# Packed attention and two dense layers: the second stage in blocks of 496, 496, 496, 320 and 496

## The chip, the cores and the metric

The kernel runs on one core of a Trainium2 chip. The metric is the device time of the program in microseconds. Before the change it is 1392.48 us, the median of three runs (1389.37 to 1394.6).

## What is computed

An attention over 32 packed positions, and behind it two feed-forward layers one after the other, all in float32 accuracy:

```python
p_packed = sm_attn(p, k, v)              # 8 batches, 8 heads, 32 packed rows, 576 tokens, 64 wide
out = sm_attn(q, p_packed, p_packed)     # 576 tokens against the 32 packed rows
x = out -> (4608 tokens, 512)
h = x @ w_in;  x = max(0.01*h, h) @ w_out              # first layer, 512 -> 2048 -> 512
h = x @ w_in2; x = h*sigmoid(1.702*h) @ w_out2         # second layer
```

The weights arrive as float64 and are turned into float32 on the chip.

## The kernel before, in words

Four stages follow one another, and in each TensorE has a long stream of matmuls.

- **First stage** (L563 to L600): attention, and the first activations g1 = leaky relu of x times w_in1. Per batch of 576 tokens there are 16 row groups of 128 features in two halves of 288 tokens; each is six matmuls (L369), then one activation on ScalarE (L378) into a ring of tiles g (L377), four activations to a tile, and one store of the tile to memory (L382). The ring has four buffers. In the last batch no attention work is left.
- **Second stage** (L603 to L698): y = g1 times w_out1. It is done as a Strassen product: seven products instead of eight, over token halves i and feature halves h. The tokens go in five blocks; a block (t0, n) covers 2n tokens, its halves n each. Per block the seven products run in the order of PRODUCTS (L42), each over eight row groups f; a step is one (block, product, f) and issues six matmuls of n columns (L693): two output columns times three terms, since each operand is split into a rounded high part and a low rest (high x high, high x low, low x high).
- **Third stage**: the second layer's activations, in the same manner with six blocks of 768 tokens (L727).
- **Fourth stage**: the second layer's output, again in five blocks (L840), in the order 480, 480, 480, 480, 384.

What sets the order around the change is an agenda (L122 to L145): `at(step, ...)` puts work on a step, `side(step)` issues it there, ahead of the step's matmuls. Each engine works through its own instructions in that order. In the second stage the agenda holds:

- the raw tiles of g1, loaded through SP's queue (L454 to L463), one buffer for each of their names, those of the first block in the last batch of the first stage (L591 to L593);
- the split of every second row group pair: a cast on ScalarE (L499) four steps ahead, the subtraction on VectorE (L140) three steps ahead, into three rotating slots (ROLL, L468); in a slot the high and low parts lie at offsets that depend on n (L496);
- the Strassen combinations of raw tiles on VectorE (L475 to L483), 16 a block, and the evacuation of the products (L516 to L547), copies on ScalarE and five additions on VectorE a block, with four stores of y a block (L611);
- the splits of w_out1's weights, 18 halves in the first block (L442 to L452, L557);
- sixteen conversions of w_in2 to float32 with its combinations (L166 to L196, called at L675): each loads three pieces, works on ScalarE, VectorE (L159, L162, L178 to L182) and POOL (L163), and stores one (L184). A conversion with start s loads in step s and does the rest in steps s + 6 to s + 15, the addition on POOL in s + 8;
- at the end, the first loads and splits for the third stage (y_block, L677), which take over the conversions' buffers: loads in step 240, first use in step 249.

Blocks of the second stage take 56 steps each: the fourth has steps 168 to 223, the fifth 224 to 279.

The parts that the diff touches:

Of the kernel before, what the change touches and what calls it, by code (L numbers as in the profile page):

```python
# [9 lines left out]
F32 = mybir.dt.float32  # L10
# [8 lines left out]
B, H, S, D, J = 8, 8, 576, 64, 32  # L19
# [8 lines left out]

WIDE = 480
ROW = 512  # L30
SLOT = 4 * ROW + 128
BLOCKS = {"b": [(0, 384), (768, 480), (1728, 480), (2688, 480), (3648, 480)],
          "d": [(0, 480), (960, 480), (1920, 480), (2880, 480), (3840, 384)]}
# [45 lines left out]
def packed_attention_moe_moe_kernel(tc, qT, kT, vm, vt, pT, w_in1, w_out1, w_in2, w_out2, out):  # L79
# [31 lines left out]
    with ExitStack() as ctx:  # L111
# [262 lines left out]
        def relu(b, f, hf, t):  # L374
            g = b, f // 2
            if g not in g1t:
                g1t[g], made[g] = pa.tile([P, 2, S], F32, tag="g", name=f"g1_{b}_{f}", bufs=4), 0  # L377
            nc.scalar.activation(g1t[g][:, f % 2, hf * TH:hf * TH + TH], t[:, :TH], AF.Prelu, alpha=0.01)  # L378
            made[g] += 1
            if made[g] == 4:  # L380
                f -= f % 2
                nc.sync.dma_start(g1[f:f + 2, :, b * S:b * S + S].rearrange("f p t -> p f t"), g1t.pop(g))  # L382
# [71 lines left out]
        def load_raw(blk, i, h, fp, nm, g):  # L454
            if blk < NBK:
                home, tag = "dr", f"r{i}{h}{fp}" if i == h else f"r10{fp}"
                if nm == "d":
                    home, tag = ("cy", f"y{fp}") if i != h else ("d" if h else "d0", f"r{i}{h}{fp}")
                t0, n = BLOCKS[nm][blk]
                t = pools[home].tile([P, 2, WIDE], F32, tag=tag, name=f"{nm}r_{blk}_{i}{h}{fp}")[:, :, :n]  # L460
                f0, t0 = NJ * h + 2 * fp, t0 + n * i
                nc.sync.dma_start(t, g[f0:f0 + 2, :, t0:t0 + n].rearrange("f p t -> p f t"))
                raws[blk, i, h, fp] = t  # L463
# [7 lines left out]
        def prepare(nm, g, steps=steps, home_of=split_home):  # L471
# [14 lines left out]
            def high(k, blk, p, f):  # L486
# [7 lines left out]
                else:  # L494
                    t = pools[home].tile([P, SLOT], F32R, tag=tag, name=f"{nm}a_{blk}_{p}_{f}")
                    hi, lo = (bass_rows(t[:, o:], n) for o in ((32, 2 * ROW + 96) if n == WIDE else (0, 2 * ROW)))  # L496
                for c in range(2):
# [18 lines left out]
        def evacuate(k, blk, p, bank, shape, store, home=None):  # L516
            def tile_(what):
                if home:
                    outs[what] = home[:, "uv".index(what), :, :shape[1]]
                else:  # L520
                    outs[what] = pools["d"].tile([P, 2, WIDE], F32, tag=what[0], name=f"{what}_{blk}")[:, :, :shape[1]]
                return outs[what]
# [92 lines left out]
        def y_block(early, steps, blk):  # L615
# [4 lines left out]
            def load():  # L620
                for i, j in ((0, 0), (1, 0), (1, 1), (0, 1)):
# [7 lines left out]
                    else:  # L629
                        home, tag = ("d", "yq") if blk == 0 else ("cy", f"y{2 * i + j}")  # L630
                        q[i, j] = pools[home].tile([P, 2, HB if blk == 0 else WIDE], F32, tag=tag, name=f"yq_{blk}_{i}{j}")[:, :, :HB]
                    nc.sync.dma_start(q[i, j], yT[2 * j:2 * j + 2, :, t0 + HB * i:t0 + HB * i + HB].rearrange("d p t -> p d t"))
# [41 lines left out]
        later_weights(lambda n: "w5" if n < 8 else "d", wo1c, "wo1", 0)  # L674
        combined("wi2", [42 + 23 * i // 2 for i in range(16)], 6)  # L675
        last = 7 * NJ * (NBK - 1)
# [135 lines left out]
        def store_out(blk, i, h, t, columns=(0, 1)):  # L812
            n = BLOCKS["d"][blk][1]
            if 0 in columns:
# [3 lines left out]
                else:  # L818
                    outs["rows"] = pools["d"].tile([P, 2, WIDE], F32, tag="rows", name=f"rows_{blk}_{i}{h}")[:, :, :n]
            for c in columns:  # L820
# [9 lines left out]
        for k, (blk, p, f) in enumerate(last_steps, LATER):  # L830
            if k == LATER + 4:
                uv = pools["cs"].tile([P, SLOT], F32, tag="wj", name="uv")
                uv = uv[:, :4 * WIDE].rearrange("p (i c w) -> p i c w", i=2, c=2)
            side(k)
# [65 lines left out]
```

## Time and profile before

| | before |
|---|---|
| median of three runs | 1392.48 us |
| profiled execution, span | 3422.4 us |
| TensorE busy in it | 3415.1 us |
| VectorE busy | 1064.6 us |
| ScalarE busy | 786.4 us |
| POOL busy | 89.7 us |
| DMA | 302.48 MB, 88 GB/s over the span |

The profile is one execution, taken by the hardware profiler; the page gives its span and no further time for it. Its span is 2.46 times the median of the runs, and readers should keep the two apart: a duration of the profile isn't at once a duration of the timed run. Rows name a line of the kernel, an engine, the operation and its tiles, out <- in; "128x960" is partitions by elements. Busy time is the time in which an engine had an instruction in work. SPq is SP's queue of DMA issues; "to landing" is the time from an issue until its data have arrived. The mean of one matmul in a group covers its overlap with the next, so busy time over count is what one costs in a stream. A window's row gives, for a stretch in us from the span's start, the busy time of each engine with its instructions in brackets, then the granted TensorE clock (PEclk, 1.00 is the 2.4 GHz level), the mean share of the 16 DMA engines that was busy and the GB/s; PEld is TensorE's weight load.

### The profile page before, as it was taken

How to read it: one execution, taken by the hardware profiler on the slowest of the kernel's cores; microseconds unless marked ns; L12 is line 12 of the kernel's file. 1: busy time of each engine (PE TensorE's matmuls, PEld its weight loads, DVE VectorE, ACT ScalarE, POOL GpSimd, SP SyncE). 2: the span in 40 equal slices, each digit the busy share in tenths (PEclk: the TensorE clock that was granted, in tenths of full speed). 3: DMA queues.
4: the chain of work that ended last, by engine and by line, in shares of the span. 5: the costliest groups of instructions: out<-in, count | busy, mean ns of one | idle time of the engine just before them, and what ended most of it. 6: DMA issues, size and time to landing. Idle time of an engine off the chain costs nothing.

```text
span 3422.4 us, 23306 instructions
## 1 busy us (share of the span) xinstructions
PE 3415.1 (100%) x8746; PEld 2461.0 (72%) x8746; DVE 1064.6 (31%) x1548; ACT 786.4 (23%) x1363; POOL 89.7 (3%) x71
## 2 busy tenths in 40 slices
PE   9999999999999999999999999999999999999999
PEld 7788888887666666666777777777766666666677
DVE  5233333233333333332322222321123333233332
ACT  4222222222112111111322222222222111111111
POOL 2000000000000000000000000000000000000000
DMA  6233333433222222211223332322231213031211
GB/s 247 92 133 131 132 131 104 138 111 100 64 86 64 83 78 62 93 45 58 97 87 110 104 106 94 106 96 74 94 122 54 69 29 86 23 86 29 66 32 19
DMA packets 283249, 302.48 MB, mean 88 GB/s; under 512 B 88576, under 2 KB 246272, under 8 KB 283136
## 3 DMA queue, kind: packets, MB, share of 16 engines
q1 hardware_dynamic: 280736, 300.71, 27.4%
q8 instruction: 68, 1.11, 0.1%
q10 hardware_dynamic: 2400, 0.30, 0.1%
q14 instruction: 45, 0.37, 0.0%
HBM read 184.55 MB, written 116.39 MB: 88 GB/s over the span
## 4 chain that ended last, share of the span: by engine, by line
PE 100%; issue 0%; POOL 0%; DVE 0%; ACT 0%; POOLq 0%
PE y L693 26%; PE h L727 26%; PE sum L840 19%; PE h L369 15%; PE first L840 8%; PE m L243 2%; PE s L243 1%; PE keep L389 1%; PE pp L301 1%; PE t L284 1%; PE tr L286 0%; PE t L310 0%; DVE rows L822 0%; POOL ident masks.py:199 0%; ACT ppk L313 0%
## 5 line engine op out<-in xcount | busy, mean ns | idle before, releaser
L727 PE MATMUL h<-ya,wj 128*128 128x384 f32 x2016 | 900.6, 679 | 0.0
L727 PEld LDWEIGHTS h<-ya,wj 128*128 128x128 f32 x2016 | 704.8, 352 | 195.7 <-issue 173.7
L693 PE MATMUL y<-ba,wo 128*128 128x480 f32 (+1 forms) x1080 | 579.9, 769 | 0.0
L369 PEld LDWEIGHTS h<-a,m 128*128 128x128 f32 x1536 | 493.5, 363 | 64.2 <-issue 51.0
L369 PE MATMUL h<-a,m 128*128 128x288 f32 x1536 | 523.3, 565 | 0.0
L693 PEld LDWEIGHTS y<-ba,wo 128*128 128x128 f32 x1080 | 379.6, 352 | 199.1 <-issue 197.2
L840 PE MATMUL sum<-da,wo 128*128 128x480 f32 (+1 forms) x840 | 452.3, 769 | 0.0
L840 PEld LDWEIGHTS sum<-da,wo 128*128 128x128 f32 x840 | 295.1, 352 | 155.5 <-issue 154.0
L693 PE MATMUL y<-ba,wo_early 128*128 128x480 f32 (+1 forms) x600 | 322.7, 768 | 0.0
L140 DVE TENSOR_TENSOR ba<-br,ba 128x960 fp32r<-128x960 f32 (+1 forms) x140 | 156.5, 1118 | 491.3 <-ACT ba L499 491.2
L140 DVE TENSOR_TENSOR da<-dr,da 128x960 fp32r<-128x960 f32 (+1 forms) x139 | 155.0, 1115 | 489.2 <-ACT da L499 489.2
L693 PEld LDWEIGHTS y<-ba,wo_early 128*128 128x128 f32 x600 | 211.0, 352 | 110.3 <-issue 108.9
L499 ACT CAST da<-dr 128x960 fp32r<-128x960 f32 (+1 forms) x139 | 133.3, 961 | 681.9 <-PE sum L840 432.3
L499 ACT CAST ba<-br 128x960 fp32r<-128x960 f32 (+1 forms) x140 | 134.5, 961 | 649.8 <-PE y L693 569.9
L378 ACT ACTIVATE g<-h 128x288 f32<-128x288 f32 x256 | 105.1, 411 | 455.9 <-PE h L369 427.5
L840 PE MATMUL sum<-da,wo_early 128*128 128x480 f32 (+1 forms) x360 | 193.8, 769 | 0.0
L840 PEld LDWEIGHTS sum<-da,wo_early 128*128 128x128 f32 x360 | 126.7, 352 | 66.4 <-issue 65.4
L840 PE MATMUL first<-da,wo 128*128 128x480 f32 (+1 forms) x240 | 129.9, 769 | 0.0
L749 DVE TENSOR_TENSOR g<-v,h 128x384 f32<-128x384 f32 x48 | 26.6, 554 | 331.4 <-PE h L727 331.4
L840 PE MATMUL first<-da,wo_early 128*128 128x480 f32 (+1 forms) x228 | 123.0, 766 | 0.0
L840 PEld LDWEIGHTS first<-da,wo 128*128 128x128 f32 x240 | 84.5, 353 | 43.8 <-issue 43.1
L840 PEld LDWEIGHTS first<-da,wo_early 128*128 128x128 f32 x228 | 79.9, 351 | 42.0 <-issue 41.0
(129 smaller groups left out, 1633.4 us busy)
## 6 DMA issues: line engine op xcount, KB each, us to landing
g_scratch<-g SPq DMA_DIRECT2D x64, 576.0 KB, 3.0
g_scratch<-g SPq DMA_DIRECT2D x96, 384.0 KB, 2.8
br<-g_scratch SPq DMA_DIRECT2D x64, 480.0 KB, 3.9
dr<-g_scratch SPq DMA_DIRECT2D x64, 480.0 KB, 3.7
stage<-wi_scratch SPq DMA_DIRECT2D x72, 256.0 KB, 2.8
wo_scratch<-b_wo SPq DMA_DIRECT2D x32, 448.0 KB, 4.1
k<-in_kT_dram SPq DMA_DIRECT2D x16, 576.0 KB, 4.9
q<-in_qT_dram SPq DMA_DIRECT2D x16, 576.0 KB, 4.8
```

Source lines behind the costliest of these rows:

```text
L140: at(step + 1, lambda: nc.vector.tensor_sub(*rest))
L243: nc.tensor.matmul(tiles[par][32 * i:32 * i + 32, :n], lhsT=lhsT(r, i, par), rhs=rhs(r, i), start=True, stop=True)
L284: nc.tensor.transpose(t[par][:, P * k:P * k + P], e[:, par, P * k:P * k + P], ident)
L301: nc.tensor.matmul(t[32 * i:32 * i + 32, D * par:D * par + D], lhsT=et[:n, par, k, 32 * i:32 * i + 32], rhs=v[:n, i // 2, k, c0:c0 + D], s ...
L369: nc.tensor.matmul(t[:, :TH], lhsT=m[:, ws, par, o:o + P], rhs=a[:, xs, par, :], start=(k == 0), stop=(k == 5))
L378: nc.scalar.activation(g1t[g][:, f % 2, hf * TH:hf * TH + TH], t[:, :TH], AF.Prelu, alpha=0.01)
L389: nc.tensor.matmul(keep[:, :P], lhsT=ident, rhs=ident, start=True, stop=True)
L499: nc.scalar.copy(hi, src)
L693: nc.tensor.matmul(acc[BANK[p]][:, c, :n], lhsT=w[:, ws, P * c:P * c + P], rhs=x[xs], start=(p in OPENS and f + m == 0), stop=(f == NJ - 1 ...
L727: nc.tensor.matmul(to, lhsT=w[:, ws, COMBO[p], P * kk:P * kk + P], rhs=x[:, xs, kk, :], start=(p in UNIT_OPENS and kk + s == 0), stop=(kk ...
L749: nc.vector.tensor_add(g[1][:, HB:], v, d)
L840: nc.tensor.matmul(column_of(acc4[BANK[p]], c)[:, :n], lhsT=w[:, ws, c], rhs=x[xs], start=(p in OPENS and f + m == 0), stop=(f == NJ - 1 a ...
```

## The change

The second stage's blocks become 496, 496, 496, 320, 496 instead of 384, 480, 480, 480, 480 tokens per half, with tiles of 496 where they are the second stage's and 480 where they are the fourth's. The offsets of the parts in a slot go by n > 384 instead of n = 480. The last four conversions start in steps 181, 194, 207 and 220 instead of 180, 191, 203 and 214. The ring of tiles for the first activations has three buffers instead of four.

```diff
--- before.py
+++ after.py
@@ -26,10 +26,10 @@
 TB = 768
 HB = TB // 2
 
-WIDE = 480
+WIDE = {"b": 496, "d": 480}
 ROW = 512
 SLOT = 4 * ROW + 128
-BLOCKS = {"b": [(0, 384), (768, 480), (1728, 480), (2688, 480), (3648, 480)],
+BLOCKS = {"b": [(0, 496), (992, 496), (1984, 496), (2976, 320), (3616, 496)],
           "d": [(0, 480), (960, 480), (1920, 480), (2880, 480), (3840, 384)]}
 NBK = 5
 SCALE = 1.0 / 8.0
@@ -374,7 +374,7 @@
         def relu(b, f, hf, t):
             g = b, f // 2
             if g not in g1t:
-                g1t[g], made[g] = pa.tile([P, 2, S], F32, tag="g", name=f"g1_{b}_{f}", bufs=4), 0
+                g1t[g], made[g] = pa.tile([P, 2, S], F32, tag="g", name=f"g1_{b}_{f}", bufs=3), 0
             nc.scalar.activation(g1t[g][:, f % 2, hf * TH:hf * TH + TH], t[:, :TH], AF.Prelu, alpha=0.01)
             made[g] += 1
             if made[g] == 4:
@@ -457,7 +457,7 @@
                 if nm == "d":
                     home, tag = ("cy", f"y{fp}") if i != h else ("d" if h else "d0", f"r{i}{h}{fp}")
                 t0, n = BLOCKS[nm][blk]
-                t = pools[home].tile([P, 2, WIDE], F32, tag=tag, name=f"{nm}r_{blk}_{i}{h}{fp}")[:, :, :n]
+                t = pools[home].tile([P, 2, WIDE[nm]], F32, tag=tag, name=f"{nm}r_{blk}_{i}{h}{fp}")[:, :, :n]
                 f0, t0 = NJ * h + 2 * fp, t0 + n * i
                 nc.sync.dma_start(t, g[f0:f0 + 2, :, t0:t0 + n].rearrange("f p t -> p f t"))
                 raws[blk, i, h, fp] = t
@@ -493,7 +493,7 @@
                     hi, lo = (bass_rows(x, n) for x in (hi, lo))
                 else:
                     t = pools[home].tile([P, SLOT], F32R, tag=tag, name=f"{nm}a_{blk}_{p}_{f}")
-                    hi, lo = (bass_rows(t[:, o:], n) for o in ((32, 2 * ROW + 96) if n == WIDE else (0, 2 * ROW)))
+                    hi, lo = (bass_rows(t[:, o:], n) for o in ((32, 2 * ROW + 96) if n > HB else (0, 2 * ROW)))
                 for c in range(2):
                     ga[blk, p, f + c] = hi[:, c], lo[:, c]
                 nc.scalar.copy(hi, src)
@@ -518,7 +518,7 @@
                 if home:
                     outs[what] = home[:, "uv".index(what), :, :shape[1]]
                 else:
-                    outs[what] = pools["d"].tile([P, 2, WIDE], F32, tag=what[0], name=f"{what}_{blk}")[:, :, :shape[1]]
+                    outs[what] = pools["d"].tile([P, 2, WIDE["b"]], F32, tag=what[0], name=f"{what}_{blk}")[:, :, :shape[1]]
                 return outs[what]
             if p == 1 and home:
                 u = tile_("u")
@@ -628,7 +628,7 @@
                         q[i, j] = q[home, tag][:, o:o + 2 * HB].rearrange("p (a b) -> p a b", a=2)
                     else:
                         home, tag = ("d", "yq") if blk == 0 else ("cy", f"y{2 * i + j}")
-                        q[i, j] = pools[home].tile([P, 2, HB if blk == 0 else WIDE], F32, tag=tag, name=f"yq_{blk}_{i}{j}")[:, :, :HB]
+                        q[i, j] = pools[home].tile([P, 2, HB if blk == 0 else WIDE["d"]], F32, tag=tag, name=f"yq_{blk}_{i}{j}")[:, :, :HB]
                     nc.sync.dma_start(q[i, j], yT[2 * j:2 * j + 2, :, t0 + HB * i:t0 + HB * i + HB].rearrange("d p t -> p d t"))
 
             def one(i):
@@ -672,7 +672,7 @@
 
         first_raws("b", g1)
         later_weights(lambda n: "w5" if n < 8 else "d", wo1c, "wo1", 0)
-        combined("wi2", [42 + 23 * i // 2 for i in range(16)], 6)
+        combined("wi2", [42 + 23 * i // 2 for i in range(12)] + [181, 194, 207, 220], 6)
         last = 7 * NJ * (NBK - 1)
         y_block(last + 16, [last + k for k in (25, 27, 30, 35, 42, 49, 54)], 0)
         side_until(0)
@@ -816,7 +816,7 @@
                     rows = pools["conv"].tile([P, 4 * HB], F32, tag="cx", name=f"rows_{blk}_{i}{h}")
                     outs["rows"] = rows[:, :2 * n].rearrange("p (c w) -> p c w", c=2)
                 else:
-                    outs["rows"] = pools["d"].tile([P, 2, WIDE], F32, tag="rows", name=f"rows_{blk}_{i}{h}")[:, :, :n]
+                    outs["rows"] = pools["d"].tile([P, 2, WIDE["d"]], F32, tag="rows", name=f"rows_{blk}_{i}{h}")[:, :, :n]
             for c in columns:
                 rows = outs["rows"][:, c]
                 nc.vector.transpose(rows, column_of(t, c)[:, :n])
@@ -830,7 +830,7 @@
         for k, (blk, p, f) in enumerate(last_steps, LATER):
             if k == LATER + 4:
                 uv = pools["cs"].tile([P, SLOT], F32, tag="wj", name="uv")
-                uv = uv[:, :4 * WIDE].rearrange("p (i c w) -> p i c w", i=2, c=2)
+                uv = uv[:, :4 * WIDE["d"]].rearrange("p (i c w) -> p i c w", i=2, c=2)
             side(k)
             x, w = ga.pop((blk, p, f)), wt[p, f // 4][:, :, f % 4].rearrange("p s (c w) -> p s c w", c=2)
             n = BLOCKS["d"][blk][1]
```

## Rows read from the trace of the kernel before

**Rows 1.** The page: span, busy time of each engine, the chain that ended last.
```profile
span 3422.4 us, 23306 instructions
...
PE 3415.1 (100%) x8746; PEld 2461.0 (72%) x8746; DVE 1064.6 (31%) x1548; ACT 786.4 (23%) x1363; POOL 89.7 (3%) x71
...
PE 100%; issue 0%; POOL 0%; DVE 0%; ACT 0%; POOLq 0%
```

**Rows 2.** Stage two by block: us, PE, PEld, DVE, ACT, POOL, PEclk, DMA, GB/s.
```profile
717.15:867.21 150.06, 150.06 (x337) 117.59 (x337) 57.97 (x73) 36.55 (x52) 1.29 (x1) 1.00 0.32 103
867.21:1054.76 187.55, 187.55 (x337) 118.28 (x336) 64.78 (x79) 36.04 (x41) 8.83 (x5) 1.00 0.23 76
1054.76:1242.31 187.55, 187.55 (x337) 118.19 (x336) 64.05 (x75) 36.06 (x41) 8.83 (x5) 1.00 0.24 76
1242.31:1429.86 187.55, 187.55 (x337) 118.34 (x336) 65.16 (x79) 36.03 (x41) 8.04 (x5) 1.00 0.25 79
1429.86:1617.41 187.55, 187.55 (x337) 118.07 (x336) 65.61 (x66) 35.39 (x40) 0.00 (x0) 1.00 0.13 42
```

**Rows 3.** Groups by shape, PE, L693's two shapes | busy us, mean ns.
```profile
L693 PE MATMUL y<-ba,wo 128*128 128x480 f32 x864 | 483.3, 791 | 0.0
...
L693 PE MATMUL y<-ba,wo 128*128 128x384 f32 x216 | 96.7, 680 | 0.0
```

**Rows 4.** Windows by product of the first block of stage two.
```profile
717.15:738.59 21.44, 21.44 (x50) 16.80 (x50) 8.55 (x10) 3.64 (x5) 0.00 (x0) 1.00 0.47 151
738.59:760.02 21.43, 21.43 (x50) 17.08 (x49) 8.52 (x10) 5.07 (x7) 0.00 (x0) 1.00 0.23 69
760.02:781.46 21.44, 21.44 (x49) 16.66 (x48) 8.85 (x11) 6.11 (x9) 0.00 (x0) 1.00 0.33 103
781.46:802.90 21.44, 21.44 (x50) 16.57 (x49) 7.15 (x9) 5.42 (x8) 0.00 (x0) 1.00 0.00 0
802.90:824.34 21.44, 21.44 (x50) 16.92 (x49) 10.58 (x13) 5.41 (x8) 0.00 (x0) 1.00 0.26 87
824.34:845.78 21.44, 21.44 (x49) 17.02 (x48) 7.11 (x9) 6.11 (x9) 0.00 (x0) 1.00 0.56 181
845.78:867.21 21.43, 21.43 (x49) 16.54 (x48) 7.21 (x11) 4.79 (x6) 1.29 (x1) 1.00 0.42 133
```

**Rows 5.** Groups by shape, VectorE, then ScalarE, stage two | busy us, mean ns.
```profile
L140 DVE TENSOR_TENSOR ba<-br,ba 128x960 fp32r<-128x960 f32 x112 | 129.7, 1158 | 416.1 <-ACT ba L499 416.1
L140 DVE TENSOR_TENSOR ba<-br,ba 128x768 fp32r<-128x768 f32 x27 | 25.9, 958 | 73.6 <-ACT ba L499 73.4
...
L140 DVE TENSOR_TENSOR wo<-wo 128x512 fp32r<-128x512 f32 x18 | 11.7, 685 | 0.0
L162 DVE SCALAR_TENSOR_TENSOR raw_wi<-raw_wi 128x512 uint32<-128x512 uint32 x16 | 11.0, 689 | 0.3
L159 DVE TENSOR_SCALAR raw_wi<-raw_wi 128x512 uint32<-128x512 uint32 x16 | 6.9, 429 | 1.0 <-ACT raw_wi L156 1.0
...
L179 DVE TENSOR_TENSOR b_wi<-b_wi 128x128 f32<-128x128 f32 x16 | 4.7, 292 | 0.6
...
L499 ACT CAST ba<-br 128x960 fp32r<-128x960 f32 x112 | 111.2, 993 | 558.5 <-PE y L693 496.9 <-issue 61.6
```

**Rows 6.** End of stage one: its window; lines L378 and L382; DMA issues there.
```profile
645.70:717.15 71.45, 71.45 (x241) 63.19 (x239) 11.05 (x16) 21.23 (x48) 0.00 (x0) 1.00 0.42 140
...
L378 ACT ACTIVATE g<-h x256: 404/411/418, 48.0 to 717.3; 128x288 f32<-128x288 f32 x128
...
L382 SPq DMA_DIRECT2D g_scratch<-g x64: 359/377/517, 64.0 to 717.8; - x64
...
DMA to landing us min/median/max: 2.9/3.0/6.6
...
g_scratch<-g SPq DMA_DIRECT2D x8, 576.0 KB, 3.3
br<-g_scratch SPq DMA_DIRECT2D x12, 384.0 KB, 4.8
```

## The prediction

> **What bounds the kernel now.** I read the page first. TensorE is busy for 3415.1 of a span of 3422.4 us, and the chain that ended last is 100% PE [rows 1]. In the profiled execution nothing but the matmul stream counts. Its span is 2.46 times the median of the timed runs (3422.4 / 1392.48), and the page gives no other time for it. So the sum is made on that execution and carried over: if every matmul shrinks alike, a profiled microsecond is worth 0.407 us in the timed runs.
>
> Next the windows, one for each block of the second stage [rows 2]. The block of 384 tokens takes 150.06 us, each block of 480 takes 187.55. Divided by the width that is 0.3908 and 0.3907 us per token of width. There is no fixed part: a block costs its width and nothing else. The per-shape groups agree, 483.3 us / 864 = 559 ns for 480 columns and 96.7 / 216 = 448 ns for 384 [rows 3]. Every window shows a granted clock of 1.00, the 2.4 GHz level [rows 2], so no gated stretch explains the slow matmuls.
>
> Then the other engines in the same windows. VectorE is busy 57.97 us in the first block and 64.05 to 65.61 in the others, ScalarE 35 to 37 [rows 2]. Against 150 or 187 us that is far from bounding. But the timed runs went through the same work 2.46 times faster, and VectorE's and ScalarE's instructions don't shrink with TensorE's. Carried over, the first block gives TensorE 150.06 x 0.407 = 61.1 us against VectorE's 57.97, and a block of 480 has 76.3 against 65. So VectorE is close behind TensorE, closest in the first block, and there the change works. The seven products of that block show where VectorE's load gathers: 10.58 us in the fifth, 7.1 to 8.9 in the others [rows 4].
>
> **The change, part by part.**
>
> *Block widths, TensorE.* The widths sum to 384 + 4 x 480 = 2304 before and 4 x 496 + 320 = 2304 after; each block issues 336 matmuls either way. At 0.3907 us per token of width the stage costs 900.2 us in the profiled execution before and after: difference 0. This is the term that sits on the path.
>
> *Block widths, VectorE and ScalarE.* Each block has 28 splits (L140), 16 combinations (L475 to L483) and 5 additions of the evacuation (L532 to L546), 49 instructions over twice the width. L140's takes 1158 ns at 960 elements and 958 at 768 [rows 5], and I take that for all 49, so 1.04 ns per element: 1191 at 992, 825 at 640. The first block therefore gains 49 x 0.233 = 11.4 us, each block going from 480 to 496 gains 1.6, the one that falls to 320 loses 16.3. The instruction count and the elements are the same in sum. The renamed widths and the test n > 384 leave the fourth stage's tiles and every slot's kind of offset as they were: 0. ScalarE's cast goes the same way (993 ns at 960 [rows 5], some 1020 at 992); its 37 us a block stay off the path.
>
> *Conversions.* The last four of the 16 start at steps 181, 194, 207, 220 instead of 180, 191, 203, 214. Counting steps, one whole conversion leaves the fourth block for the fifth. On VectorE it costs 0.429 + 0.689 + 4 x 0.29 = 2.3 us [rows 5]. It also takes its three loads and one store on SP's queue and its addition on POOL with it, later by 1 to 6 steps. Its last store now falls in step 235, and the next user of its buffers, the loading for the third stage, issues in step 240. Should that cover fail, that load waits on SP's queue with the loads behind it, and the first reader comes in step 249. I take 0.
>
> *VectorE per block after* (from [rows 2] and the two terms above): 69.4, 66.4, 65.7, 46.6, 69.5 us, sum 317.6 as before. At the carried-over pace TensorE has 78.9 us for a width of 496 and 50.9 for 320. TensorE stays longer in every block: gain 0.
>
> *What if TensorE is faster in the timed runs than 0.407 of the profile, with waits making up the rest?* No row shows that pace, so I bound it from both sides. Let c be TensorE's time per token of width. A block costs the longer of c x width and VectorE's time. The carried-over c is 0.159; VectorE's time per token of width is 0.151, 0.135, 0.133, 0.136, 0.137 before and 0.140, 0.134, 0.132, 0.146, 0.140 after. Above 0.151 the change gives 0. Between 0.146 and 0.151 only the old first block waits for VectorE, and the gain grows to 2.1 us. From there to 0.140 the new block of 320 waits too, and the gain grows slowly to 11.37 - 64 x 0.140 = 2.4 us. Below that the new first and fifth blocks wait as well: at 0.137 the change loses 5.5 - 6.2 = 0.7 us. With TensorE free of charge both kernels cost VectorE's 317.6: 0 again. So by whole blocks the change is worth between 0.7 us lost and 2.4 us gained, whatever the pace.
>
> The Trainium skill has a pace in "TensorE: Matmul & The Clock Gate", section "Back-to-back issue gap": N/2.4 + 2.5 ns for a warm matmul. The 559 ns of [rows 3] at a granted clock of 1.00 don't agree with its 202.5; no row here shows it for the timed runs. By it the old first block would have 54.6 us of matmuls against 57.97, the new fourth 45.6 against 46.6, and the sum would be a gain of 2.4 us, an estimate of 1390.1.
>
> *Three buffers instead of four (L377).* A buffer is filled by four activations, stored, and free once the store has landed. In the last eighth of the first stage, where nothing else runs, a fill takes 71.45 / 8 = 8.93 us in the profile [rows 6], 3.6 carried over. Fill, activation 0.41, issue 0.38 and landing 3.0 make 7.4 us against 3 x 3.6 = 10.9 until its next use; with the longest landing of the trace, 6.6 us [rows 6], 11.0. I take 0. The cover is the time in which the other two buffers fill; without it the activation waits, then TensorE for its bank. The upper end is a rival below. A gain is excluded: a ring with fewer buffers waits no less.
>
> *Larger first loads.* Twelve raw tiles of the first block are fetched in that same eighth, 384 KB each [rows 6], now 496: 1.3 MB more. There DMA ran at a share of 0.42 and 140 GB/s, so 333 GB/s when full: 4.1 us more transfer, after 0.42 x 71.45 = 30 us. At the timed pace that eighth lasts 29 us. The first block of the second stage absorbs it (48 us of transfer at share 0.32 [rows 2], in 61 before and 79 after), and the last of these tiles are first read in step 9. I take 0, bounds 0 and +4.1; a gain is excluded, since no byte less moves.
>
> *Sum.* 0 at the carried-over pace, up to 2.4 gained; I take 1.5, because the first block is where both bounds meet and some of the timed run must be waiting. 1392.5 - 1.5 = **1391.0 us**, no change. A measurement of this kernel tells about 0.5% (7 us) from nothing.
>
> **Rivals.**
>
> *A: the old first block stalls by product, not by block.* VectorE can work only a few steps ahead, since the split values have three slots. If no lead carries over at all, each product costs the longer of the two. At c = 0.140 a product of 384 has 7.69 us; the excesses of [rows 4] add to 0.86 + 0.83 + 1.16 + 2.89 = 5.7 us, at 0.130 to 8.1. If the wider block hides all that and the block of 320 pays nothing, the time is 1385. For it: the weight splits (18 of 0.69 us) all fall in this block. Against it: products of 7.1 stand on both sides of the 10.58, and the block of 320 has VectorE at 0.146 of its own. Chance 0.2.
>
> *B: the end of the first stage (slower).* With transfers filling that eighth, stores land late, and with three buffers the activation waits for them. The price per tile is a third of what fill + 0.79 + landing exceeds three fills. At a fill of 3.6 us, 7 us over 8 tiles needs landings of 9.1 us; at 2.9 us (c = 0.140), 7.6. With 4.1 us of transfers exposed as well it gives up to +9: 1399 to 1401. For it: DMA demand of 30 us in 29. Against it: a median landing of 3.0, the rest of the stage has slower fills, and loads queued late aren't needed until the second stage. Chance 0.14.
>
> *C: it does only what the widths say.* TensorE bounds every block in the timed runs too; 1392.5. This is the forecast's own lower end, counted with it: 0.66 together.
>
> **How the numbers follow.** Forecast 0.66, 1388 to 1394 by itself. Range: down to 1381 for A beyond its price and the unshown handoffs, up to 1400 for B's middle. Faster by over 0.5% needs 1385.5 or less: A, 0.20. Slower needs 1399.4 or more: B, 0.14. Same: 0.66.
>
> **What would show it.** In a profile of the same kind: windows of about 194 us for the blocks of 496 and 125 for 320; VectorE near 69, 66, 66, 47, 69; four POOL additions of the second stage in the fourth block and one in the fifth; activations of L378 waiting only for TensorE. If TensorE shows idle time before L693 there, or L378 waits for a store, A's or B's mechanism is at work. The prediction is wrong if the time leaves 1385.5 to 1399.4; a profile in which matmuls run at another pace would settle c.

## The result and the profile after

The changed kernel is **slower by 17.8 us**: a median of 1409.83 us (1406.27 to 1411.17, four runs) against 1391.99 (1389.37 to 1394.6, four runs), ratio 1.0122 with a 95% interval of 1.0102 to 1.0142. The prediction said no change, 1391.0, and its range ended at 1400.

The profiled execution after ran at the pace of the timed runs (it is the one of 1406.27 us), and so did a second profiled execution of the kernel before, called *before again* below (experiment 1). They can be compared directly; the first profile of before, with its span of 3422.4 us [rows 1], can't. The two spans differ by 14.9 us and not by 17.8, since the profiled execution after is the fastest of its four runs. The page of after, span and busy time:

```profile
span 1404.5 us, 23312 instructions
...
PE 1369.8 (98%) x8746; PEld 1218.8 (87%) x8746; DVE 1056.2 (75%) x1548; ACT 767.2 (55%) x1363; POOL 94.8 (7%) x71
```

The same lines of before again. VectorE is busy for 76% of the span, not the 31% of [rows 1]:

```profile
span 1389.6 us, 23306 instructions
...
PE 1363.6 (98%) x8746; PEld 1225.7 (88%) x8746; DVE 1052.7 (76%) x1548; ACT 768.4 (55%) x1363; POOL 97.9 (7%) x71
```

The windows of after (columns as in [rows 2]): first the last batch of stage one, then the five blocks of stage two, with widths 496, 496, 496, 320, 496:

```profile
293.00:324.80 31.80, 30.36 (x243) 26.47 (x241) 9.55 (x15) 18.85 (x46) 0.00 (x0) 1.00 1.02 377
...
324.80:401.20 76.40, 75.66 (x337) 63.17 (x337) 70.33 (x74) 43.48 (x55) 1.30 (x1) 1.00 0.66 222
401.20:477.20 76.00, 76.00 (x337) 63.08 (x336) 67.86 (x78) 36.96 (x41) 11.06 (x5) 1.00 0.60 195
477.20:553.20 76.00, 76.00 (x337) 63.08 (x336) 67.14 (x77) 36.31 (x41) 9.03 (x5) 1.00 0.55 170
553.20:614.90 61.70, 54.55 (x337) 52.24 (x336) 50.09 (x77) 26.69 (x39) 6.57 (x4) 0.94 0.59 192
614.90:691.70 76.80, 75.56 (x338) 62.80 (x337) 67.90 (x69) 37.30 (x42) 2.14 (x1) 1.00 0.38 129
```

The same windows of before again, widths 384 and four times 480:

```profile
294.50:323.90 29.40, 29.26 (x242) 26.40 (x241) 10.45 (x15) 19.75 (x48) 0.00 (x0) 1.00 1.04 379
...
323.90:383.70 59.80, 58.87 (x338) 58.29 (x337) 55.26 (x68) 36.87 (x53) 1.81 (x1) 1.00 0.73 240
383.70:458.20 74.50, 74.15 (x339) 62.61 (x338) 65.68 (x84) 36.23 (x41) 12.68 (x5) 1.00 0.64 207
458.20:531.30 73.10, 73.10 (x337) 62.95 (x336) 66.95 (x78) 36.13 (x41) 8.95 (x5) 1.00 0.62 202
531.30:604.90 73.60, 73.60 (x337) 62.82 (x337) 66.15 (x80) 36.11 (x41) 9.19 (x5) 1.00 0.61 201
604.90:678.60 73.70, 73.70 (x336) 62.65 (x335) 64.25 (x66) 35.55 (x40) 0.94 (x1) 1.00 0.32 108
```

TensorE still costs its width and nothing else where it isn't kept waiting: 76.0 / 496 = 0.1532 us per token, 73.6 / 480 = 0.1533. Five blocks without a wait would be 2304 x 0.1533 = 353.2 us. Before again has 354.7, after 366.9. Of the 13.7 us too many, 12.6 lie in one block: a width of 320 is 49.0 us of matmuls and took 61.7. TensorE is idle there for 7.15 us, and its matmuls take 54.55, which is 5.5 us more than 49.0. The last three stretches of that block show where part of those 5.5 us is, in the column before the last two, the granted clock:

```profile
593.00:601.00 8.00, 7.24 (x39) 7.24 (x40) 7.58 (x13) 2.32 (x4) 0.02 (x1) 0.79 0.70 202
601.00:609.00 8.00, 6.24 (x40) 5.75 (x40) 3.00 (x5) 3.54 (x6) 0.18 (x1) 0.99 1.06 377
609.00:614.90 5.90, 5.90 (x32) 5.79 (x31) 5.08 (x9) 2.04 (x2) 1.11 (x1) 0.72 1.05 392
```

After TensorE had stood idle, part of the following stretch was granted at the 1.2 GHz level: means of 0.79 and 0.72, worth some 0.21 x 8.0 + 0.28 x 5.9 = 3.3 us (an estimate from these rows). The wide blocks show 1.00. So a wait can be paid for twice. Not each one is: in the four windows of 8 us before these, from 561 to 593, TensorE was idle for 4.6 us in all, and the clock stayed at 1.00.

What TensorE waited for is in the waits of that block (us in total, times, longest):

```profile
ACT raw_wi L155 <- DMA raw_wi<-in_w_in_dram: 8.5, 4, 3.9
DVE raw_wi L159 <- ACT raw_wi L156: 8.3, 3, 4.3
PEld y L693 <- DVE ba L140: 7.6, 7, 2.6
PE y L693 <- DVE ba L140: 5.8, 6, 2.3
```

Read from the bottom: TensorE waits for split values of VectorE (5.8 us), and, in the top line, ScalarE waits for the loads of a conversion (8.5 us). Before again has, in its second to fourth blocks together, 3.4 us of ScalarE's waits for such loads and 0.3 us of TensorE's for VectorE. The timeline of one conversion in the narrow block, the one that starts in step 181, ties them together (start, duration, engine, instruction; in square brackets the wait before it):

```profile
562.76 1.78 POOL L163 TENSOR_TENSOR b_wi<-raw_wi 128x512 int32<-128x512 int32 x1 [11.15 <-DVE raw_wi L162]
...
567.46 0.29 DVE L182 TENSOR_TENSOR b_wi<-b_wi 128x128 f32<-128x128 f32 x1
...
567.82 0.56 SPq L184 DMA_DIRECT2D wi_scratch<-b_wi  x1
...
568.55 1.53 SPq L173 DMA_DIRECT2D raw_wi<-in_w_in_dram  x2
570.13 0.60 SPq L174 DMA_DIRECT2D raw_wi<-in_w_in_dram  x1
...
574.00 0.67 ACT L155 ACTIVATE raw_wi<-raw_wi 128x512 int32<-128x512 uint32 x1 [2.03 <-DMA raw_wi<-in_w_in_dram]
...
575.12 2.12 ACT L499 CAST ba<-br 128x640 fp32r<-128x640 f32 x3
...
576.33 0.82 DVE L140 TENSOR_TENSOR ba<-br,ba 128x640 fp32r<-128x640 f32 x1
...
577.20 2.02 PE L693 MATMUL y<-ba,wo 128*128 128x320 f32 x12 [0.62 <-DVE ba L140]
...
577.88 1.75 POOL L163 TENSOR_TENSOR b_wi<-raw_wi 128x512 int32<-128x512 int32 x1 [13.35 <-DVE raw_wi L162]
...
578.40 1.93 DVE L140 TENSOR_TENSOR ba<-br,ba 128x640 fp32r<-128x640 f32 x1
...
580.38 0.85 PE L693 MATMUL y<-ba,wo 128*128 128x320 f32 x4 [1.16 <-DVE ba L140]
```

The previous conversion ends on VectorE at 567.75 (L182); its store (L184) waits for that on SP's queue, and in the changed kernel the next loads stand right behind that store, because 181 is the start before, 168, plus 13, the step of the store. They issue at 568.55 to 570.73. Their buffer had been free since the addition before ended, at 562.76 + 1.78 = 564.54; the place behind the store held them for 4.0 us. The next three conversions are the same: their loads issue 4.0, 5.6 and 3.1 us after the addition that frees the buffer, and 0.6 to 0.7 us after the store. ScalarE reaches L155 six steps after the planned load, waits 2.03 us, and the casts (L499) that feed TensorE stand behind it in ScalarE's order. VectorE's splits come late, TensorE waits. Then POOL's addition makes the next split 1.93 us instead of 0.82, and TensorE waits again. Six steps are 8.1 us in a block of 496 (76.0 / 56 x 6) and 5.3 us in one of 320.

### The profile page after: what moved, and what is told of

It reads as the page before. It is cut to its first block, busy times and chain, and to the rows that moved or that the text cites. A ratio compares the mean times of both kernels' runs of the same rounds, so it can differ in the third digit from the quotient of the medians.

```text
span 1404.5 us, 23312 instructions
## 1 busy us (share of the span) xinstructions
PE 1369.8 (98%) x8746; PEld 1218.8 (87%) x8746; DVE 1056.2 (75%) x1548; ACT 767.2 (55%) x1363; POOL 94.8 (7%) x71
## 5 line engine op out<-in xcount | busy, mean ns | idle before, releaser
L727 PE MATMUL h<-ya,wj 128*128 128x384 f32 x2016 | 351.4, 334 | 2.4 <-ACT h L741 1.6
L727 PEld LDWEIGHTS h<-ya,wj 128*128 128x128 f32 x2016 | 349.3, 188 | 4.4 <-ACT h L741 2.6
L369 PEld LDWEIGHTS h<-a,m 128*128 128x128 f32 x1536 | 208.2, 189 | 33.9 <-issue 13.3
L693 PE MATMUL y<-ba,wo 128*128 128x496 f32 (+1 forms) x1080 | 231.8, 376 | 5.9 <-DVE ba L140 4.5
L499 ACT CAST da<-dr 128x960 fp32r<-128x960 f32 (+1 forms) x139 | 134.1, 966 | 184.3 <-PE sum L840 121.0
L693 PEld LDWEIGHTS y<-ba,wo 128*128 128x128 f32 x1080 | 197.0, 191 | 39.9 <-DVE ba L140 5.8
L369 PE MATMUL h<-a,m 128*128 128x288 f32 x1536 | 223.3, 301 | 8.0 <-ACT g L378 2.7
L499 ACT CAST ba<-br 128x992 fp32r<-128x992 f32 (+1 forms) x140 | 134.4, 964 | 154.9 <-PE y L693 132.5
L140 DVE TENSOR_TENSOR ba<-br,ba 128x992 fp32r<-128x992 f32 (+1 forms) x140 | 168.5, 1205 | 20.9 <-ACT ba L499 18.6
L840 PE MATMUL sum<-da,wo 128*128 128x480 f32 (+1 forms) x840 | 178.7, 372 | 0.0
L840 PEld LDWEIGHTS sum<-da,wo 128*128 128x128 f32 x840 | 154.8, 187 | 22.5 <-DVE da L140 0.3
L378 ACT ACTIVATE g<-h 128x288 f32<-128x288 f32 x256 | 102.5, 419 | 84.5 <-PE h L369 60.4
L693 PE MATMUL y<-ba,wo_early 128*128 128x496 f32 (+1 forms) x600 | 127.8, 372 | 3.3 <-DVE ba L140 3.3
L693 PEld LDWEIGHTS y<-ba,wo_early 128*128 128x128 f32 x600 | 107.5, 188 | 22.6 <-DVE ba L140 4.7
```

Of the source, the lines that this page charges most:

```text
L140: at(step + 1, lambda: nc.vector.tensor_sub(*rest))
L369: nc.tensor.matmul(t[:, :TH], lhsT=m[:, ws, par, o:o + P], rhs=a[:, xs, par, :], start=(k == 0), stop=(k == 5))
L499: nc.scalar.copy(hi, src)
L693: nc.tensor.matmul(acc[BANK[p]][:, c, :n], lhsT=w[:, ws, P * c:P * c + P], rhs=x[xs], start=(p in OPENS and f + m == 0), stop=(f == NJ - 1 ...
L727: nc.tensor.matmul(to, lhsT=w[:, ws, COMBO[p], P * kk:P * kk + P], rhs=x[:, xs, kk, :], start=(p in UNIT_OPENS and kk + s == 0), stop=(kk ...
L840: nc.tensor.matmul(column_of(acc4[BANK[p]], c)[:, :n], lhsT=w[:, ws, c], rhs=x[xs], start=(p in OPENS and f + m == 0), stop=(f == NJ - 1 a ...
```

## The experiments

Theories named in the expectations: **Q**, the new starts put the loads behind the previous store; **L**, six steps of a narrow block are too short for a load, whatever the queue; **V**, VectorE itself (with POOL) is too busy; **R**, the ring of three; **M**, the larger first loads alone fill DMA; **W**, a block of 320 is slow by itself; **K**, a conversion's loads come too late for a short step, and ScalarE's casts stand in order behind them; **R2**, ring and larger first loads together; **K2**, the conversions' loop through one buffer (loads, work, addition) takes a fixed time and can't be started more often. Diffs stand against the changed kernel, or against the kernel before where that is said. Ratios are to the kernel before on the same chip.

**1. The kernel before, unchanged**, for a profile at the timed pace.

> The kernel before, unchanged, for a profile in which TensorE runs at the pace of the timed runs. Theory Q (the fourth block's conversions are loaded late, because each load now stands behind the store of the conversion before it on SP's queue): its second stage shows no block with long waits; five blocks sum to 2304 x 0.1535 = 354 us plus at most 3 us, against 367 after, and its first stage lasts as after within 1 us. Theory R (the ring of three buffers costs): its first stage, up to the first matmul of the second, is 3 to 6 us shorter than the 324.8 us after. Both may hold together, since 367 - 354 = 13 us of the 17.8 lie in the second stage.

One run of 1391.44 us, span 1389.6. Its rows stand above; its group of the wide matmuls is

```profile
L693 PE MATMUL y<-ba,wo 128*128 128x480 f32 x864 | 190.1, 380 | 0.0
```

190.1 / 864 = 220 ns, where [rows 3] has 559. Stage two takes 354.7 us by its windows, against 366.9 after. R's 3 to 6 us don't show: stage two begins at 323.9 us here and at 324.8 after. Only the last batch of stage one is longer after, 31.8 us against 29.4.

**2 and 3. Other starts in the changed kernel.** Run 2 restores the old ones, run 3 takes a spacing of 12.

```diff
-        combined("wi2", [42 + 23 * i // 2 for i in range(12)] + [181, 194, 207, 220], 6)
+        combined("wi2", [42 + 23 * i // 2 for i in range(16)], 6)
```
```diff
+        combined("wi2", [42 + 23 * i // 2 for i in range(12)] + [180, 192, 204, 216], 6)
```

> The changed kernel with the conversions back on their old steps (180, 191, 203, 214): the loads issue one or two steps before the store of the conversion before. Theory Q: most of the 12 us of the fourth block come back, 1397 to 1401 us. Rival V (VectorE and POOL are overloaded in a block of 320 tokens): a conversion more in that block, 2.3 us of VectorE and up to 1.1 us of contention with POOL's addition, so 1411 to 1414. Rival L (six steps of a narrow block are too short for a load, whatever the queue): unchanged, 1408 to 1411.

> The changed kernel with the last four conversions on 180, 192, 204, 216: as many in the fourth block as with 181, 194, 207, 220, but each load one step ahead of the store of the one before. Theory Q: 1397 to 1401 us, and ScalarE's waits for the loads (8.5 us after) fall below 3. Rival V: 1408 to 1412, nothing in the load of VectorE and POOL has changed. Rival L: 1408 to 1411.

The old starts give 1404.56 us (1.0097, 1.008 to 1.0113), the spacing of 12 1410.79 (1.0149, 1.0129 to 1.0168). Both are outside what Q expected, and most of the loss stays. L expected no change, which holds for run 3 and not for run 2; V's range holds for run 3 and fails for run 2. The narrow block's windows, run 2 and then run 3:

```profile
556.50:612.40 55.90, 52.70 (x337) 50.80 (x336) 48.62 (x76) 25.91 (x38) 6.62 (x4) 0.97 0.61 193
```
```profile
556.00:611.50 55.50, 51.44 (x337) 49.23 (x336) 50.38 (x77) 26.85 (x39) 7.08 (x4) 1.00 0.61 194
```

Here Q is right: with the loads ahead of the store the narrow block takes 55.9 and 55.5 us instead of 61.7, with as many additions on POOL in it, and ScalarE waits 3.4 and 2.4 us for loads there instead of 8.5. But the fifth block takes 80.8 and 83.1 us instead of 76.8. There ScalarE waits 5.0 and 5.3 us, at the start of the block, for the load of the last conversion, which was issued while DMA was full (share 1.06 from 605 us on, in both); the changed kernel has 2.7 us of that. So the loss moved rather than went: the two blocks together take 136.7 and 138.6 us, against 138.5. Q falls as the whole account.

**4 and 5. Two parts alone in the kernel before**: the new starts, and three buffers.

```diff
-        combined("wi2", [42 + 23 * i // 2 for i in range(16)], 6)
+        combined("wi2", [42 + 23 * i // 2 for i in range(12)] + [181, 194, 207, 220], 6)
```
```diff
-tag="g", name=f"g1_{b}_{f}", bufs=4), 0
+tag="g", name=f"g1_{b}_{f}", bufs=3), 0
```

> The kernel before, with the new steps of the conversions alone (blocks of 384 and 480, four buffers). Theory Q: each load stands behind a store here too, but six steps last 7.9 us instead of 5.3, so most of the lateness is covered: 1392 to 1397 us. Rival V: 1391 to 1393, since the block of 480 has room. Rival L: 1391 to 1393.

> The kernel before with three buffers for the first activations instead of four, and nothing else. Theory R (the ring costs at the end of the first stage, as the profiles suggest: the last batch of it takes 31.6 us after and 29.2 before): 2 to 4 us slower, 1393 to 1396, with waits of 0.7 to 1.1 us ahead of groups 239, 247, 251 and 255 of its 256. Rival M (the 1.3 MB more of first loads cause that, not the ring): 1390.5 to 1392.

1390.71 us (1.0002, 0.9987 to 1.0017) and 1391.68 (0.9998, 0.9988 to 1.0007). In blocks of 480 the same starts cost nothing, though the loads stand behind the stores there too, and the ring costs nothing with first loads of 384 KB. Each alone is as the prediction had it.

**6 and 7. The last four conversions without their loads, and left out.** In run 6 they work on the raw values of the twelfth; in run 7 the results of four earlier ones are stored twice. In both the last quarter of w_in2 isn't converted.

```diff
+            if name in ("wi2_6_0", "wi2_6_1", "wi2_7_0", "wi2_7_1"):
+                raw, v = kept
+            else:
...
```
```diff
+            twice = {"wi2_4_0": "wi2_6_0", "wi2_4_1": "wi2_6_1", "wi2_5_0": "wi2_7_0", "wi2_5_1": "wi2_7_1"}.get(name)
+            if twice:
+                nc.sync.dma_start(place(twice, scratch), b)
...
-        combined("wi2", [42 + 23 * i // 2 for i in range(12)] + [181, 194, 207, 220], 6)
+        combined("wi2", [42 + 23 * i // 2 for i in range(12)], 6)
```

> The changed kernel; the last four conversions load nothing and work on the data that the twelfth left in its buffer (the last quarter of w_in2 is not converted). All their work on ScalarE, VectorE and POOL and their stores stay. Theory K (a conversion's load, which waits for POOL's addition of the one before to free the only buffer and then for SP's queue, holds up ScalarE's queue with the casts behind it): the fourth block loses most of its waits, 1396 to 1400 us. Rival V (VectorE, POOL and their contention are too much for a block of 320 tokens): 1407 to 1411.

> The changed kernel without the last four conversions: those four results are stored twice by the conversions before them (the last quarter of w_in2 is not converted). One conversion is left in the fourth block, started at its first step. Theory K: as without the loads, 1396 to 1400 us. Rival V: the same, so this run by itself does not tell K from V, but both fall if it stays at 1404 or above: then the block's width alone stalls it, by its own raw tiles (theory W).

1399.73 us (1.0060, 1.0047 to 1.0073) and 1395.62 (1.0033, 1.0022 to 1.0044). The narrow block's windows, run 6 and then run 7:

```profile
556.60:609.40 52.80, 50.83 (x337) 49.24 (x336) 48.49 (x77) 26.89 (x39) 7.40 (x4) 1.00 0.53 169
```
```profile
555.40:608.20 52.80, 50.21 (x338) 49.33 (x337) 42.23 (x59) 23.75 (x33) 1.69 (x1) 1.00 0.57 190
```

Run 6 has all the work on ScalarE, VectorE (48.49 us) and POOL, and 8.9 of the narrow block's 12.6 us are gone. So V falls as the main cause: it is the loads. By the ratios (1.0122, 1.0060, 1.0033) the loss is 17.0 us; the loads cost 0.0062 x 1392 = 8.6 of it, the rest of the four conversions 3.8, and 4.6 remain. The 3.8 are the least certain, since the two intervals nearly meet; the narrow block takes 52.8 us in both runs, and the two profiled spans differ by 1.4. Of the 4.6, some 2 lie at the end of stage one (its last batch takes 31.8 us in run 6 and 31.4 in run 7, against 29.4; runs 9 and 10 below); in run 7's narrow block TensorE is idle for 2.6 us, and the one conversion left in it accounts for that:

```profile
ACT raw_wi L155 <- DMA raw_wi<-in_w_in_dram: 2.4, 1, 2.4
```

**8. The narrow block last**, where no conversions fall, with the old starts. It measures the width by itself, in time alone: its output isn't right, for a reason that was not followed up, and it is no version to use.

```diff
-BLOCKS = {"b": [(0, 496), (992, 496), (1984, 496), (2976, 320), (3616, 496)],
+BLOCKS = {"b": [(0, 496), (992, 496), (1984, 496), (2976, 496), (3968, 320)],
```

> The changed kernel with the blocks 496, 496, 496, 496, 320, and the conversions on their old steps: all of them lie in blocks of 496, none in the one of 320, which has the first loads and splits for the third stage instead. Theories K and V: no long waits in the fourth block, at most 3 us in the fifth; what is left to before is the ring and the first loads, 1392 to 1397 us. Theory W: the fifth block stalls by 8 us or more, 1402 or above.

1393.16 us (1.0019, 1.0009 to 1.0029), and the block of 320:

```profile
629.90:681.10 51.20, 50.32 (x336) 49.09 (x335) 48.32 (x66) 27.71 (x40) 0.00 (x0) 1.00 0.40 131
```

51.2 us, 2.2 over its width, with VectorE at 48.32. W falls: 320 is slow with conversions in it, not by itself. A last block has no raw tiles to load for a next one; run 7, whose narrow block loads them and has one conversion, closes that gap with 52.8 us.

**9 and 10. The end of stage one.** The kernel before with its narrow block last, so that the first loads are 480 KB, with four buffers (run 9) and with three (run 10).

```diff
-BLOCKS = {"b": [(0, 384), (768, 480), (1728, 480), (2688, 480), (3648, 480)],
+BLOCKS = {"b": [(0, 480), (960, 480), (1920, 480), (2880, 480), (3840, 384)],
```

> The kernel before with its blocks in the order 480, 480, 480, 480, 384, four buffers, old steps. Theory M (the larger first loads, 480 KB instead of 384 each, fill DMA at the end of the first stage): the last batch takes 30.5 us or more with four buffers too, and the whole 1392 to 1394. Theory R2 (only ring and larger loads together cost): 29.2 us as in the kernel before, and with the 384 block free of conversions 1388 to 1391.

> The same with three buffers. Theory M: equal to the run with four, within 1 us. Theory R2: the last batch takes 31 us or more and 1 to 2.5 us are lost against the run with four.

Run 9: 1387.98 us (0.9961, 0.9944 to 0.9978). Run 10: 1393.11 (1.0004, 0.9988 to 1.0019). Their last batch, run 9 and then run 10:

```profile
295.40:324.70 29.30, 29.16 (x241) 26.30 (x241) 10.27 (x15) 19.83 (x48) 0.00 (x0) 1.00 1.03 383
```
```profile
294.80:326.20 31.40, 30.01 (x242) 26.41 (x240) 9.49 (x14) 18.95 (x46) 0.00 (x0) 1.00 1.04 384
```

In the last batch larger first loads with four buffers cost nothing, three buffers with small loads cost nothing (run 5, 29.4 us), both together cost 2.1 us here and 2.4 in the changed kernel. DMA is full in all of them. The wait is there in the changed kernel's last batch; before again and run 9 show none, run 5 has 1.6 us of it:

```profile
ACT g L378 <- DMA g_scratch<-g: 5.3, 4, 2.1
```

R2 stands for the last batch. The medians of runs 9 and 10 differ by 5.1 us, more than the 1 to 2.5 expected; by the profiles 1.4 more lie in the first block of stage two (74.8 against 73.4 us) and 1.2 in stage three, and what the ring has to do with that is not shown. Run 9 is also faster than the kernel before by 0.4%; why was not followed up.

**11. Denser conversions throughout**, so that only the last two fall into the narrow block.

```diff
+        combined("wi2", [42 + 17 * i // 2 for i in range(16)], 6)
```

> The changed kernel with all sixteen conversions 8.5 steps apart, steps 42 to 169: one is left in the block of 320, and the three wide blocks before it hold six to seven each, 2 x 2.3 us of VectorE more. Theory K: a load has six wide steps, 8.2 us, before ScalarE wants it, so the wide blocks stay without waits, and the time is as without the late conversions, 1394 to 1398 us. Rival V: VectorE's 66 + 4.6 us and contention come near the 76 us of a wide block by product, 1400 or above.

1409.71 us (1.0120, 1.0103 to 1.0138): K's expectation missed, and V's met. The second and third block, wide ones, now stall; then the waits of that stretch:

```profile
404.30:484.00 79.70, 77.06 (x338) 62.38 (x336) 67.29 (x85) 38.11 (x45) 15.27 (x6) 1.00 0.59 187
484.00:565.40 81.40, 77.17 (x338) 62.77 (x338) 73.46 (x92) 38.35 (x44) 11.06 (x7) 1.00 0.60 195
```
```profile
ACT raw_wi L155 <- DMA raw_wi<-in_w_in_dram: 22.3, 7, 6.7
```

The first of them speaks against V all the same: VectorE is busy for 67.29 us in it, and for 67.86 in the changed kernel's second block, which takes 76.0 us. 8.5 steps of a wide block are 11.5 us (76.0 / 56 x 8.5). In the trace each load issues within 0.1 us of the end of the previous conversion's addition, and the additions end 9.5 to 15.2 us apart, 12.4 in the mean. So here the loads wait for the buffer and come late whatever the planned lead. K2 was formed on this, on the thought that 13 narrow steps, 11.4 us, are the same condition. In the changed kernel they are not: its loads wait for the store, with the buffer free for 3.1 to 5.6 us (timeline above).

**12. Loads ten steps ahead** for the last four conversions, the work later by four.

```diff
-                pieces(combine(f"{what}_{j}_{u}", src, to), (s, *(s + late + k for k in (0, 1, 2, 5, 6, 7, 8, 9))))
+                pieces(combine(f"{what}_{j}_{u}", src, to), (s, *(s + late + 4 * (what == "wi2" and n > 11) + k for k in (0, 1, 2, 5, 6, 7, 8, 9))))
```

> The changed kernel; the last four conversions still load on steps 181, 194, 207, 220, but do the rest ten steps later instead of six. All work stays in the same blocks but the last conversion's, and each load now issues ahead of the store of the one before. Theory K: the lead of 8.8 us covers the landing, 1396 to 1401 us, and ScalarE's wait for these loads in the block, 8.5 us after, falls below 2. Rival V: 1406 to 1411, as the work in the block is the same.

1399.14 us (1.0061, 1.0038 to 1.0084), as K has it. The narrow block's window, and the wait for loads in it, 1.9 us instead of 8.5:

```profile
553.00:607.50 54.50, 51.82 (x338) 50.85 (x336) 47.42 (x72) 26.86 (x39) 5.49 (x3) 0.97 0.59 192
```
```profile
ACT raw_wi L155 <- DMA raw_wi<-in_w_in_dram: 1.9, 1, 1.9
```

The work that is four steps later also takes one addition out of this block (three, not four), and most of the loads now stand ahead of the store, as in runs 2 and 3; the lead by itself is not separated from that. Against those two runs the gain is in the fifth block, 77.9 us instead of 80.8 and 83.1.

**13. Sixteen steps apart in the narrow block**, 14 us, longer than the loop.

```diff
+        combined("wi2", [42 + 11 * i for i in range(12)] + [179, 195, 211, 226], 6)
```

> The changed kernel with conversions 11 steps apart up to step 163 (15.0 us in a wide block) and then on 179, 195, 211, 226: 16 narrow steps are 14.1 us. The conversions' whole work stays, three or four of them in the narrow block. Theory K2 (a conversion's loop through its one buffer takes 13 to 14 us beside the other work, and a spacing shorter than that in microseconds stalls the casts queued behind it): the narrow block loses most of its waits, 1396 to 1401 us. Width alone (theory W) or the work in the narrow block (rival V): 1405 or above.

1407.06 us (1.0123, 1.0099 to 1.0147): K2's expectation missed; the number is in the range of W and V. But the narrow block's 61.5 us hold only 46.29 of VectorE's, and most of its 12.5 us too many are one wait with the slow clock behind it: 6.5 us of idle TensorE, and at most 0.50 x 5.0 = 2.5 by the clock. The windows before, in and after it, then ScalarE's wait and TensorE's:

```profile
600.00:606.70 6.70, 6.70 (x48) 6.70 (x47) 2.72 (x4) 1.45 (x2) 0.00 (x0) 1.00 1.07 385
606.80:613.50 6.70, 0.30 (x3) 0.04 (x1) 0.43 (x1) 1.81 (x4) 0.00 (x0) 0.90 1.05 372
613.60:618.60 5.00, 4.77 (x15) 4.26 (x16) 3.78 (x6) 2.60 (x3) 2.12 (x1) 0.50 0.63 205
```
```profile
ACT raw_wi L155 <- DMA raw_wi<-in_w_in_dram: 9.1, 1, 9.1
...
PE y L693 <- ACT ba L499: 6.5, 1, 6.5
```

The loads issued at 601.7 to 603.4 took 7.9 and 8.8 us to land, among the raw tiles of the next wide block that fill DMA (share 1.07, 385 GB/s). The changed kernel has that too: in its own last stretches of the narrow block DMA is at 1.05 to 1.06. So the loop isn't all: with a spacing of 14 us a load that met a full DMA was late too.

**14. The denser starts in the kernel before**, which has no narrow block among those with conversions.

```diff
-        combined("wi2", [42 + 23 * i // 2 for i in range(16)], 6)
+        combined("wi2", [42 + 17 * i // 2 for i in range(16)], 6)
```

> The kernel before, old blocks and four buffers, with conversions 8.5 steps apart, 11.1 us in its blocks of 480. Theory K2: the two blocks with six conversions wait 3 to 6 us each, 1398 to 1406 us, and ScalarE waits 10 us or more for the conversions' loads. If the width or the other parts of the change were needed for the stall: 1390 to 1393.

1409.93 us (1.0143, 1.0116 to 1.017): the direction that K2 expected, but above its range, which ended at 1406. Its second to fourth blocks, 480 wide, and the wait for loads in them:

```profile
381.70:462.00 80.30, 75.79 (x339) 61.95 (x337) 67.82 (x91) 37.46 (x45) 14.31 (x6) 1.00 0.62 196
462.00:542.00 80.00, 75.21 (x338) 62.40 (x337) 69.25 (x86) 38.03 (x44) 9.80 (x6) 1.00 0.61 200
542.00:622.70 80.70, 76.84 (x337) 64.59 (x336) 62.08 (x67) 32.69 (x35) 6.16 (x3) 0.96 0.53 174
```
```profile
ACT raw_wi L155 <- DMA raw_wi<-in_w_in_dram: 31.5, 11, 7.3
```

Nothing else of the change is in this kernel, and it loses as much as the whole change. So late loads cost that much without any narrow block. VectorE is busy for 67.82 us of the first of these blocks, against 66.95 in a block of 73.1 us of before again. What makes the loads late isn't the same: here, as in run 11, they wait for the addition, in the changed kernel for the store.

**Left open:** how the loss by late loads divides between the place behind the store, the short lead and the full DMA (runs 2, 3, 12 and 13 show each in part, none by itself). Four buffers beside tiles of 496, and a second buffer for the conversions, weren't tried.

## Why the prediction was wrong

**TensorE's widths, 0: right.** 0.1532 and 0.1533 us per token, no fixed part. The carried-over pace of 0.159 was 4% too slow. The formula of the Trainium skill ("TensorE: Matmul & The Clock Gate", "Back-to-back issue gap"), which the page gives for a warm matmul by itself, makes an estimate of 202.5 ns for 480 columns; the 220 measured here don't agree with it, and it was further off.

**VectorE per block: near, but for the narrow one.** Predicted 69.4, 66.4, 65.7, 46.6, 69.5; measured 70.3, 67.9, 67.1, 50.1, 67.9. It is below TensorE's time in every block but the narrow one. There the prediction had TensorE 4.3 us longer (50.9 against 46.6), and it is 1.1 shorter (49.0 against 50.1). Run 6 shows that this bounds only a little: 52.8 us with 48.5 of VectorE's.

**Conversions, 0: the step that failed.** The prediction counted what moves (one conversion to the fifth block, by steps) and its instructions, and named as cover only the last store, in step 235 before the loading of step 240. (A conversion's last piece, the store, falls 13 steps after its start and not 15, so this one is in step 233.) It put the wait for a load at nothing. It didn't ask what "six steps ahead" is in a block whose steps last 0.87 us instead of 1.31, nor what stands ahead of the loads on SP's queue: starts that are 13 apart put each load right behind the store of the conversion before. What the runs showed in place of the 0: ScalarE waited 8.5 us for these loads in the narrow block, the casts behind it came late, and TensorE stood idle for 7.15 us. The loads and ScalarE's place in order behind them were all in the profile of before; there 187.55 / 56 x 6 = 20 us of lead hid them. About 12 of the 17.0 us were here: 8.6 by the loads, which run 6 shows, 3.8 by the rest of those conversions, less certain.

**The bound "between 0.7 us lost and 2.4 gained, whatever the pace" was none.** It compared busy times by block. An engine that stands still in order for a load is busy with nothing, and every cast behind it is late all the same; no sum of busy times holds that.

**Three buffers, 0, and larger first loads, 0: each right alone (runs 5, 9), wrong together**, by 2.4 us in the last batch. Rival B had this mechanism, but at a price of 7 to 9 us, and it isn't what made most of the loss. The landing of 3.0 us was the wrong term: with DMA full (1.02), which B's "for it" had seen, the last eight stores took 9.1 us in the median. That is the landing that B asked for 7 us; it cost 2.4. That the time came out beyond B's 1399.4 is no point for B.

**Rival A fell.** Before again, the block of 384 took 59.8 us against 384 x 0.1533 = 58.9; there were 0.9 us to gain, not 7.

## What to carry to other kernels

A lead or a spacing that is written in steps is a time: turn it into microseconds of the shortest step it will meet, and set it against the time from issue to landing, read also where DMA is full. Ask what must happen before the load can issue at all: what stands ahead of it on its queue, and when its buffer is free. A load's first reader that stands in order ahead of other work makes that work late too, so its margin counts even where no engine is near its limit. And where a profile's span is far from the timed runs, its idle time and its slack say nothing about them; run the kernel before once more under the profiler, or leave slack out of the argument.

## What the runs showed of the hardware that was not expected

- One profiled execution of before had its 480-column matmuls at 559 ns, the next at 220, both at a granted clock of 1.00 [rows 2, 3]. The granted clock didn't show what slowed the first; the cause was not found.
- VectorE's split of 128x640 took 0.82 us alone and 1.93 us while POOL's addition ran (timeline above). The 0.82 agrees with the 0.825 that the prediction scaled.
- After 6.7 us with hardly a matmul (run 13) the granted clock of the next 5 us was 0.50, the 1.2 GHz level. The same matmul of 320 columns took 325 ns (3.9 us / 12) there and 150 ns (7.2 / 48) ahead of the wait.
